# Splitting two of the second layer's seven products into seven smaller ones

## The chip, the cores and the metric

The kernel runs on one core of one Trainium2 chip. The metric is device time in microseconds (us) of one execution; of several executions the median is taken. TensorE multiplies, VectorE (DVE in the profile) and ScalarE (ACT) work element by element and can read the matmul accumulators in PSUM, GpSimd (POOL) works on SBUF, and SyncE's queue (SPq) issues the transfers (DMAs).

## What is computed

```python
kv  = einsum('bhsd,bhse->bhde', k, v)            # 8 batches, 8 heads, 576 tokens, 64 dims
att = einsum('bhsd,bhde->bhse', q, kv)
att = att / sqrt(mean(att*att, -1) + 1e-6) * g_norm
x   = att.transpose(0, 2, 1, 3).reshape(4608, 512)
h   = (1 / (1 + exp(-(x @ w_gate)))) * (x @ w_val)   # 4608 x 1536
out = h @ w_out                                      # 4608 x 512
```

Everything is float32.

## The kernel before, in words

**Chunks and stages.** The 4608 tokens are worked in nine chunks of 512 (`G`). Chunk 0 is multiplied plainly while the weights arrive. Chunks c = 1 to 8 each go through two stages: `first_layer_fast(c)` makes h (kept transposed, twelve tiles `gv[c, f]` of 128 features x 512 tokens), `second_layer_fast(c)` multiplies h by `w_out`. Both stages use a seven-product scheme (the one of Winograd and Strassen): a 2 x 2 block product is made with seven block products in place of eight, from sums of the operands' quarters and sums of the results.

**The second layer's operands.** The tokens of a chunk are two halves `h1`, `h2` of 256, the features two groups of six tiles (`lo` = f 0 to 5, `hi` = f 6 to 11), the 512 output columns two halves `d1`, `d2`. Three sums of `w_out`'s quarters are made once (`t2w`). The sums of h (`s12`, `s4`, and one quarter of `gv` overwritten by a difference) are made per f by VectorE in `h_sum` and `h_sums` (lines 844 to 856) as the first layer ends. All these tiles are of one pool of 21 buffers (`hp`, tag `gv`), which the k and v tiles of a later batch take too (`load_late`, line 105).

**The second layer's order.** For each g of two (128 of the 256 tokens of either half), seven products of six matmuls, each of 128 features x 128 tokens against 256 columns, accumulate in PSUM banks that `take` and `give` hand round (five banks). ScalarE copies or VectorE adds each result into `o1` or `o2`, two of the four `sg` buffers (`sg_tile`, line 480, 128 x 512 each; the first layer uses the same four, two per f, in turn). `store` (line 483) writes `o2` and `o1` of g = 0 in the middle of the stage and those of g = 1 near its end. A store of 128 tokens is two DMAs on SyncE's queue. For chunks whose rows lie in batch 2 or later, tokens are kept permuted, and a DMA has the form 32 x n rows with n from 1 to 3 (line 498); before that, it is one run of up to 128 rows (line 492). After the last store, `load_late(c + 2)` issues twelve DMAs for the k and v of a later batch; they are used by `kv_mm` (line 354), nine slots into the next first layer.

**The filler.** Attention for batch c + 1 is cut into steps and put into `fill` by `spread` (line 460). Each `slot()` in the matmul stream pops one step and emits it there, so that it takes its place in its engine's queue behind what was emitted before. The first layer has 42 slots, the second 28 (two per product). In the second layer of chunks 1 to 6 the slots hold, counted from 0: at 5 a TensorE step (`u_mm`, line 395), 6 and 9 ScalarE steps, 7 and 8 VectorE sums (line 404), 10 and 11 VectorE normalisations (line 413), 12 and 13 VectorE transposes (line 420), each followed by six DMAs from `xTs` to `xT` (line 430), 14 to 17 nothing, 18 the unpacking of `x_sums(c + 1)`, and 19 to 26 its eight VectorE sums (lines 691 to 694 of 512 columns, 701 to 704 of 128), the first of which reads what the DMAs of line 430 write. Chunk 7's eight sums lie in slots 1 to 8; chunk 8 has none. For chunk 1, twelve VectorE steps that make `t2w` are inserted too, every third place.

DMAs of SyncE's queue take eight completion semaphores in turn, so a DMA is issued only when the one eight before it has landed.

Of the kernel before, what the change touches and what calls it, by code (L numbers as in the profile page):

```python
# [15 lines left out]
ALU = mybir.AluOpType  # L16
# [4 lines left out]
def kernel(  # L21
# [11 lines left out]
    nc = tc.nc  # L33

    B, H, S, HD = q.shape
    T, DM = out.shape
    DF = moe_w_gate.shape[1]
    P = 128
# [22 lines left out]
    NFT = DF // P  # L61
    G = 512
    GH = G // 2
    NG = T // G
# [40 lines left out]
    def load_late(b):  # L105


        if b >= B:
            return
        mains = {}  # L110
        for n in range(NHP):
            for name, src in (("k", k), ("v", v)):
                mains[n, name] = t = hp.tile([P, G], FP32, tag="gv", name="kv")
                nc.sync.dma_start(out=t.rearrange("p (h c) -> p h c", h=2),
                                  in_=src[b, 2 * n:2 * n + 2, 0:S4].rearrange("h (p j) d -> p h (j d)", j=NK4))
        rest = hp.tile([P, G], FP32, tag="gv", name="kv")
        for i, src in enumerate((k, v)):
            for r in range(2):
                nc.sync.dma_start(out=rest[PH * r:PH * r + PH, GH * i:GH * i + GH].rearrange("p (h d) -> p h d", d=HD),
                                  in_=src[b, NHP * r:NHP * r + NHP, S4:S].rearrange("h p d -> p h d"))  # L120
        kv_late[b] = mains, rest
# [213 lines left out]
    def slot():  # L335
        if fill:
            fill.popleft()()
# [122 lines left out]
    def spread(steps, at):  # L460

        n = 0
        for engine, step in steps:
            while engine == DVE and n < 7 * NF2 and n % 7 not in at:
                fill.append(idle)
                n += 1
            fill.append(step)
            n += 1

    def flush():  # L470
        while fill:
            fill.popleft()()

    gv = {}
# [5 lines left out]
    def sg_tile():  # L480
        return sb.tile([P, G], FP32, tag="sg", name="sg", bufs=4)

    def store(c, t, ot, cols=slice(0, DM), queues=(nc.sync,)):

        r0 = i = 0
        while r0 < P:
            b, s = divmod(G * c + P * t + r0, S)
            rows = out[S * b:S * b + S, cols]
            if b < 2:
                j, p = divmod(s, NP)  # L490
                n = min(P - r0, NP - p)
                queues[i % len(queues)].dma_start(out=rows.rearrange("(p j) d -> j p d", j=NJ)[j, p:p + n],
                                                  in_=ot[r0:r0 + n, cols])
            else:
                half, c0 = divmod(s, S // 2)
                r, c0 = divmod(c0, XC)
                n = min(P - r0, XC - c0)
                queues[i % len(queues)].dma_start(
                    out=rows.rearrange("(r p g i) d -> i r g p d", p=QB, g=JH, i=2)[half, r, c0 // QB:(c0 + n) // QB],
                    in_=ot[r0:r0 + n, cols])  # L500
            r0 += n
            i += 1
# [7 lines left out]
    def bank(i):  # L510
        return (psum_mm if i < 2 else psum).tile([P, 512], FP32, tag=f"mm{i}", name="mm")
# [3 lines left out]
    def mm0_ps():  # L515
        return bank(next(turns0) % 2)

    def mm_ps():
        return bank((2, 3, 0, 1)[next(turns) % 4])

    def at_ps():
        return psum.tile([P, NQ, 512], FP32, tag="at", name="at")
# [4 lines left out]
    def take():  # L527
        i = free.popleft()
        return i, bank(i)[:, 0:GH]

    def give(i):
        free.append(i)

    def early(n):

        shared = []

        def ps(kind):
            if kind == "q":
                return shared[0]  # L540
            t = psum0.tile([P, 2, 512], FP32, tag="kq" if kind == "kv" else f"ux{n % 2}", name="two")
            if kind == "kv":
                shared.append(t)
                return t[:, :, JH * P:]
            return t
        return ps
# [33 lines left out]
    a = [attention(n, early(n)) for n in range(NE)]  # L580
# [19 lines left out]
    for token in order.split():  # L600
        name = token.rstrip("0123456789.")
        n = [int(i) for i in token[len(name):].split(".")]
        f = n[0]
        if name == "b":
            if f not in blks:
                if f == 3:
                    psum_ctx.__exit__(None, None, None)
                    psum = ctx.enter_context(tc.tile_pool(name="psum", bufs=1, space=bass.MemoryType.PSUM))
                    ps = (mm_ps(), mm_ps())
                else:  # L610
                    ps = (mm0_ps() if f else warm, mm0_ps())
# [29 lines left out]
    for f in range(4, NFT):  # L641
        if f == NFT - 1:
            last = at_ps()
# [6 lines left out]
    ps = [mm_ps() for _ in range(G // P)]  # L650
# [22 lines left out]
    NF2 = NFT // 2  # L673
    DH = DM // 2
    h1, h2 = slice(0, GH), slice(GH, G)
    tt = nc.vector.tensor_tensor
    sx, tw, s12, s4 = {}, {}, {}, {}
# [171 lines left out]
    def h_sums(c, f):  # L849
# [5 lines left out]
        tt(out=one[:, h2], in0=one[:, h1], in1=one[:, h2], op=ALU.subtract)  # L855
        tt(out=s4[c, f], in0=two[:, h1], in1=s[:, h2], op=ALU.subtract)

    def second_layer_fast(c):
        b = {(j, n): w2[:, NF2 * (j - 1):NF2 * j, DH * (n - 1):DH * n] for j in (1, 2) for n in (1, 2)}
        d1, d2 = slice(0, DH), slice(DH, DM)  # L860
        for g in range(2):
            t1, t2 = slice(P * g, P * g + P), slice(GH + P * g, GH + P * g + P)
            (i_a, pa), (i_b, pb) = (take() for _ in range(2))

            last = (c, g) == (NG - 1, 1)
            parts = [slice(0, DH // 2), slice(DH // 2, DH)] if last else [slice(0, DH)]

            def product(ps, hs, ws, new):
                for f in range(NF2):
                    nc.tensor.matmul(ps, hs(f), ws[:, f, :], start=(new and f == 0), stop=(f == NF2 - 1),  # L870
                                     skip_group_check=True)
                    if f % 3 == 2:
                        slot()

            product(pa, lambda f: gv[c, f][:, t1], b[1, 1], True)
            o2 = sg_tile()
            nc.scalar.copy(out=o2[:, d1], in_=pa)
            product(pb, lambda f: s12[c, f][:, t2], t2w[2], True)
            o1 = sg_tile()
            tt(out=o1[:, d2], in0=pb, in1=o2[:, d1], op=ALU.add)  # L880
            product(pa, lambda f: gv[c, f + NF2][:, t1], b[2, 1], False)
            nc.scalar.copy(out=o1[:, d1], in_=pa)
            if last:
                store(c, g, o1, d1)
            product(pb, lambda f: gv[c, f][:, t2], t2w[3], False)
            tt(out=o2[:, d2], in0=pb, in1=o2[:, d1], op=ALU.add)
            pcs = []
            for x in parts:
                i_c, pc = take()
                pc = pc[:, 0:x.stop - x.start]  # L890
                pcs.append((i_c, pc))
                product(pc, lambda f: s12[c, f][:, t1], t2w[1][:, :, x], True)
                o2x = o2[:, DH + x.start:DH + x.stop]
                tt(out=o2x, in0=pc, in1=o2x, op=ALU.add)
            product(pb, lambda f: gv[c, f + NF2][:, t2], t2w[4], False)
            tt(out=o2[:, d1], in0=pb, in1=o2[:, d1], op=ALU.add)
            store(c, 2 + g, o2)
            give(i_a)
            give(i_b)
            for (i_c, pc), x in zip(pcs, parts):  # L900
                give(i_c)
                product(pc, lambda f: s4[c, f][:, t1], b[2, 2][:, :, x], False)
                y = slice(DH + x.start, DH + x.stop)
                tt(out=o1[:, y], in0=pc, in1=o1[:, y], op=ALU.add)
                if last:
                    store(c, g, o1, y, (nc.sync, nc.scalar))
            if not last:
                store(c, g, o1)
            if g == 1:
                load_late(c + 2)  # L910

    def sums_of(c):
        if c < NG:
            fill.append(lambda: fill.extendleft(reversed(x_sums(c))))
# [17 lines left out]
    t2w = {i: sums.tile([P, NF2, DH], FP32, name=f"t2w{i}", bufs=1) for i in (2, 3, 4)}  # L932
# [14 lines left out]
    for c in range(1, NG):  # L947
        if c + 1 < B:
            steps = feed(c + 1)
            if c == 1:  # L950

                i = 4
                while w2_sums:
                    steps.insert(i, (DVE, w2_sums.popleft()))
                    i += 3
            spread(steps, (1, 2, 3, 4, 5) if c == 1 else (2, 3, 4, 5))
        first_layer_fast(c)
        sums_of(c + 1)
        second_layer_fast(c)
        flush()  # L960
# [30 lines left out]
```

## Time and profile before

| | us |
|---|---|
| median of 3 runs | 1078.0 (1076.03 to 1078.93) |
| the profiled execution, its own time | 1075.73 |
| its span, first to last instruction | 1073.9 |
| a second layer (chunks 2 to 5), TensorE busy without a gap over 150 ns | 38.3 |
| a second layer of chunk 8, which has no filler | 36.5 |
| VectorE busy in a second layer (chunks 2 to 5) | 17.2 |
| GpSimd busy in a second layer (chunks 2 to 5) | 4.5 |

A line of the profile names an engine, a source line, an operation, what it writes and reads, and the shapes. In the timeline each line has start and duration in us, and in brackets the idle time of that engine before it and what ended it. One matmul of float32 appears as two MATMUL records.

### The profile page before, as it was taken

The numbers are of one execution on the slowest core, as the hardware profiler recorded it, in microseconds if no ns is written. First come the engines' busy times: TensorE is split into PE (matmuls) and PEld (weight loads), VectorE is DVE, ScalarE is ACT, GpSimd is POOL, SyncE is SP. The second block draws the span as 40 slices with busy tenths as digits, with TensorE's granted clock in tenths as the row PEclk, the third lists the DMA queues.
The fourth block names the chain that finished last, engine by engine and source line by source line (L and its number), as shares of the span: only waits on it lengthen the run. The fifth ranks groups of instructions, "written<-read, shape, count | busy, mean of one in ns | idle before, by whom it ended". The sixth has DMA issues, their size and how long they took to land.

```text
span 1073.9 us, 19464 instructions
## 1 busy us (share of the span) xinstructions
PE 1062.2 (99%) x7514; PEld 882.4 (82%) x7514; DVE 712.0 (66%) x1461; ACT 309.0 (29%) x737; POOL 442.1 (41%) x630
## 2 busy tenths in 40 slices
PE   8999999999999999999999999999999999999997
PEld 7544448888888888888888888888888888888886
DVE  4897767894579547863778357945786388628841
ACT  4654323331243113320433134312431122112210
POOL 0000035880367216640666046713663077307800
PEclk9999999999999999999999999999999999999999
DMA  9944710002400141012301140014001200010001
GB/s 259 254 157 157 244 29 22 24 17 60 119 12 13 45 128 36 12 35 62 100 23 34 42 120 13 25 45 137 13 12 27 58 2 1 2 38 1 1 1 40
DMA packets 69115, 64.96 MB, mean 60 GB/s; under 512 B 23712, under 2 KB 63008, under 8 KB 69024
## 3 DMA queue, kind: packets, MB, share of 16 engines
q1 hardware_dynamic: 68768, 63.69, 21.1%
q8 instruction: 60, 0.98, 0.4%
q14 instruction: 31, 0.25, 0.1%
q10 hardware_dynamic: 256, 0.03, 0.1%
HBM read 47.19 MB, written 9.44 MB: 53 GB/s over the span
## 4 chain that ended last, share of the span: by engine, by line
PE 97%; DVE 1%; DMA 1%; SPq 0%; issue 0%; ACT 0%; DVEq 0%
PE mm L728 46%; PE mm L870 27%; PE mm L732 7%; PE mm L556 7%; PE mm L653 4%; PE at L395 2%; PE at L354 1%; PE at L556 1%; DMA q<-in_q_dram 1%; PE two L291 0%; PE two L261 0%; PE mm L634 0%; PE two L318 0%; PE two L272 0%; PE at L360 0%; SPq L97 0%
## 5 line engine op out<-in xcount | busy, mean ns | idle before, releaser
L720 POOL TENSOR_TENSOR tw<-gv 128x256 f32<-128x256 f32 x192 | 156.2, 823 | 232.1 <-DVE w L202 145.0
L728 PE MATMUL mm<-xT,tw 128*128 128x256 f32 x768 | 198.4, 381 | 0.0
L728 PE MATMUL mm<-sx,tw 128*128 128x256 f32 x768 | 197.4, 380 | 0.0
L802 POOL TENSOR_TENSOR sg<-sg 128x256 f32<-128x256 f32 x48 | 35.6, 742 | 341.1 <-ACT sg L801 340.9
L720 POOL TENSOR_TENSOR tw<-gv,tw 128x256 f32<-128x256 f32 x192 | 155.0, 828 | 0.0
L728 PEld LDWEIGHTS mm<-xT,tw 128*128 128x128 f32 x768 | 137.3, 190 | 17.5 <-issue 2.9
L728 PEld LDWEIGHTS mm<-sx,tw 128*128 128x128 f32 x768 | 134.9, 191 | 12.4
L773 DVE TENSOR_TENSOR gv<-gv,sg 128x256 f32<-128x256 f32 x192 | 108.7, 585 | 0.0
L728 PE MATMUL mm<-sx,gv 128*128 128x256 f32 x384 | 91.2, 380 | 0.0
L728 PE MATMUL mm<-xT,gv 128*128 128x256 f32 x384 | 90.8, 379 | 0.0
L870 PE MATMUL mm<-w,gv 128*128 128x256 f32 x384 | 89.1, 381 | 0.7 <-DVE gv L773 0.7
L870 PE MATMUL mm<-t2w,gv 128*128 128x256 f32 x384 | 88.7, 381 | 0.0
L870 PE MATMUL mm<-w,s 128*128 128x256 f32 (+1 forms) x408 | 88.3, 367 | 0.0
L764 ACT ACTIVATE sg<-sg 128x256 f32<-128x256 f32 x96 | 40.0, 416 | 151.0 <-DVE sg L763 150.9
L739 ACT COPY sg<-mm 128x256 f32<-128x256 f32 x96 | 35.8, 373 | 162.7 <-PE mm L728 160.9
L870 PEld LDWEIGHTS mm<-w,gv 128*128 128x128 f32 x384 | 72.5, 190 | 12.2 <-DVE gv L773 2.5
L870 PEld LDWEIGHTS mm<-w,s 128*128 128x128 f32 x408 | 74.1, 190 | 9.4
L728 PEld LDWEIGHTS mm<-xT,gv 128*128 128x128 f32 x384 | 72.9, 190 | 10.4 <-issue 0.5
L728 PEld LDWEIGHTS mm<-sx,gv 128*128 128x128 f32 x384 | 72.5, 190 | 10.0
L870 PEld LDWEIGHTS mm<-t2w,gv 128*128 128x128 f32 x384 | 72.4, 190 | 10.0
L556 PE MATMUL mm<-xT,gv 128*128 128x512 f32 x176 | 77.4, 594 | 0.0
L745 DVE TENSOR_TENSOR gv<-mm,sg 128x256 f32<-128x256 f32 x96 | 37.0, 413 | 41.2 <-PE mm L728 37.8
(120 smaller groups left out, 1548.4 us busy)
## 6 DMA issues: line engine op xcount, KB each, us to landing
q<-in_q_dram SPq DMA_DIRECT2D x24, 288.0 KB
st<-in_moe_w_gate_dram SPq DMA_DIRECT2D x12, 512.0 KB
st<-in_moe_w_val_dram SPq DMA_DIRECT2D x12, 512.0 KB
st<-in_moe_w_out_dram SPq DMA_DIRECT2D x12, 512.0 KB
kv<-in_k_dram SPq DMA_DIRECT2D x24, 256.0 KB
kv<-in_v_dram SPq DMA_DIRECT2D x24, 256.0 KB
out_dram<-sg SPq DMA_DIRECT2D x23, 192.0 KB
xT<-xTs SPq DMA_DIRECT2D x48, 72.0 KB
```

The source lines that it names most:

```text
L395: nc.tensor.matmul(u[HD * e:HD * e + HD, r, o:o + HD], qTs[QB * r:QB * r + QB, (n0 + which) % 2, c:c + PH], kvq[QB * r:QB * r + QB, (n0 + ...
L556: nc.tensor.matmul(self.ps[i], w[("wg", "wv")[i], self.f][:, m, :], xT[self.c][:, m, :], start=(m == 0), stop=(m == NMT - 1), skip_group_c ...
L653: nc.tensor.matmul(ps[t], gv[0, f][:, P * t:P * t + P], w["wo", f], start=(f == 0), stop=(f == NFT - 1), skip_group_check=True)
L720: nc.gpsimd.tensor_tensor(out=tw[f, i], in0=b[in0], in1=b[in1] if isinstance(in1, tuple) else tw[f, in1], op=ALU.subtract)
L728: nc.tensor.matmul(ps, wt[:, m, :], xs[:, m, :], start=(new and m == 0), stop=(m == NK - 1), skip_group_check=True)
L732: nc.tensor.matmul(ps, wt, xs, start=new, stop=True, skip_group_check=True)
L739: nc.scalar.copy(out=d["sg"][:, h2], in_=d["pa"])
L745: tt(out=d["h"][:, h1], in0=d["pb"], in1=d["sg"][:, h2], op=ALU.add)
L764: nc.scalar.activation(out=d["sg"][:, h2], in_=d["sg"][:, h2], func=AF.Sigmoid)
L773: tt(out=d["h"][:, h], in0=d["h"][:, h], in1=d["sg"][:, h], op=ALU.mult)
L802: nc.gpsimd.tensor_tensor(out=g2[:, h1], in0=g2[:, h1], in1=g2[:, h2], op=ALU.add)
L870: nc.tensor.matmul(ps, hs(f), ws[:, f, :], start=(new and f == 0), stop=(f == NF2 - 1), skip_group_check=True)
```

## The change

Of the seven products per stage, two are no longer made as one: the one that went into `o1[:, d1]` (`gv` hi, tokens of `h1`, with the quarter `b[2, 1]` of `w_out`), and the one that went into `o2[:, d1]` (`gv` hi, tokens of `h2`, with `t2w[4]`). Each is split once more in seven (`split`), on blocks of 3 feature tiles x 128 tokens x 128 columns, so it takes 21 matmuls of 128 columns for both g together in place of 12 of 256.

The sums that this needs are made per chunk by `sums2`: of the two quarters of `w_out` on GpSimd (`tw4`, `tw2_`, twelve operations of 128 x 128 each), of h on VectorE (`sa4`, `sa2`, twelve each). They overwrite parts of `gv` and `s12` tiles whose last reader has been emitted.

The other five products are now emitted in pairs over g, so that all four of `o1`, `o2` are alive until the splits, which come last: `split(o2)`, the stores of both `o2`, `split(o1)`, the stores of both `o1`, then `load_late`. In the last chunk the `d2` halves of `o1` are stored before the last split, and the `d1` halves in pieces after it. Slots per stage stay 28: 0 to 19 in the ten large products, 20 to 23 in `split(o2)`, 24 to 27 in `split(o1)`. The `t2w` steps of chunk 1 are inserted every second place.

```diff
+    N3 = NF2 // 2
+    d1, d2 = slice(0, DH), slice(DH, DM)
+    tok = [slice(P * i, P * i + P) for i in range(G // P)]
+    def sums2(engine, x, out, weights):
+        o = dict(zip((1, 2, 4, 3), out))
+        if weights:
+            ops = ((1, (1, 2), (1, 1)), (2, (2, 2), 1), (4, (2, 1), 2), (3, (2, 2), (1, 2)))
+        else:
+            o[3] = x[2, 1]
+            ops = ((1, (2, 1), (2, 2)), (2, 1, (1, 1)), (3, (1, 1), (2, 1)), (4, (1, 2), 2))
+        for i, in0, in1 in ops:
+            for j in range(N3):
+                u0, u1 = (x[n][j] if isinstance(n, tuple) else o[n][j] for n in (in0, in1))
+                engine.tensor_tensor(out=o[i][j], in0=u0, in1=u1,
+                                     op=ALU.add if i == 1 and not weights else ALU.subtract)
+        return o
...
-        for g in range(2):
...
-            product(pa, lambda f: gv[c, f + NF2][:, t1], b[2, 1], False)
-            nc.scalar.copy(out=o1[:, d1], in_=pa)
...
-            product(pb, lambda f: gv[c, f + NF2][:, t2], t2w[4], False)
-            tt(out=o2[:, d1], in0=pb, in1=o2[:, d1], op=ALU.add)
-            store(c, 2 + g, o2)
...
+        for g in pair:
+            i_, pa = take()
+            product(pa, of(gv, lo, g), b[1, 1], True)
+            o2[g] = sg_tile()
+            nc.scalar.copy(out=o2[g][:, d1], in_=pa)
+            give(i_)
+        tw4 = sums2(nc.gpsimd, b4, thirds(of(gv, lo, 0) + of(gv, lo, 1)), True)
+        for g in pair:
+            i_b[g], pb[g] = take()
+            product(pb[g], of(s12, lo, 2 + g), t2w[2], True)
+            o1[g] = sg_tile()
+            nc.scalar.copy(out=o1[g][:, d1], in_=o2[g][:, d1])
+            tt(out=o1[g][:, d2], in0=pb[g], in1=o2[g][:, d1], op=ALU.add)
+        sa4 = sums2(nc.vector, a4, thirds(of(s12, lo, 2) + of(s12, lo, 3))[:3], False)
+        for g in pair:
+            product(pb[g], of(gv, lo, 2 + g), t2w[3], False)
+            tt(out=o2[g][:, d1], in0=pb[g], in1=o2[g][:, d1], op=ALU.add)
+            give(i_b[g])
+        sa2 = sums2(nc.vector, a2, thirds(of(gv, lo, 2) + of(gv, lo, 3))[:3], False)
+        for g in pair:
+            i_c[g], pc[g] = take()
+            product(pc[g], of(s12, lo, g), t2w[1], True)
+            tt(out=o2[g][:, d2], in0=pc[g], in1=o2[g][:, d1], op=ALU.add)
+        tw2_ = sums2(nc.gpsimd, b2, thirds(of(s12, lo, 0) + of(s12, lo, 1)), True)
+        for g in pair:
+            product(pc[g], of(s4, lo, g), b[2, 2], False)
+            tt(out=o1[g][:, d2], in0=pc[g], in1=o1[g][:, d2], op=ALU.add)
+            give(i_c[g])
+        def split(o, x, a, sa, w_, tw_, done=None):
+            (i_d, pd), (i_e, pe), (i_f, pf), (i_h, ph) = (take() for _ in range(4))
...
+            small(pd, a[1, 1], w_[1, 1], True)
+            add(o[0][:, l], pd)
+            small(pf, a[1, 2], w_[2, 1], True)
+            add(o[0][:, l], pf)
+            slot()
+            small(pd, sa[2], tw_[2], False)
+            add(o[0][:, r], pd)
+            small(pe, sa[1], tw_[1], True)
+            add(o[1][:, r], pe)
+            slot()
+            small(pd, sa[3], tw_[3], False)
+            y = o[1][:, x].rearrange("p (n c) -> p n c", n=2)
+            tt(out=y, in0=y, in1=pd.unsqueeze(1).to_broadcast([P, 2, P]), op=ALU.add)
+            small(ph, a[2, 2], tw_[4], True)
+            add(o[1][:, l], ph)
+            slot()
+            if done:
+                done()
+            small(pe, sa[4], w_[2, 2], False)
+            add(o[0][:, r], pe)
+            slot()
...
+        split(o2, d1, a4, sa4, b4, tw4)
+        for g in pair:
+            store(c, 2 + g, o2[g])
+        if ends:
+            for g in pair:
+                store(c, g, o1[g], d2)
+            split(o1, d1, a2, sa2, b2, tw2_, lambda: [store(c, 1, o1[1], d1), store(c, 0, o1[0], tok[0])])
+            store(c, 0, o1[0], tok[1], (nc.sync, nc.scalar))
+        else:
+            split(o1, d1, a2, sa2, b2, tw2_)
+            for g in pair:
+                store(c, g, o1[g])
+        load_late(c + 2)
...
-                    i += 3
+                    i += 2
```

More of the change, by code (lines that the diff above doesn't have):

```diff
@@ L858, in second_layer_fast @@
     def second_layer_fast(c):
         b = {(j, n): w2[:, NF2 * (j - 1):NF2 * j, DH * (n - 1):DH * n] for j in (1, 2) for n in (1, 2)}
-        d1, d2 = slice(0, DH), slice(DH, DM)
-        for g in range(2):
[L862 to L870, printed above, removed]
-                                     skip_group_check=True)
[L872 to L880, printed above, removed]
-            product(pa, lambda f: gv[c, f + NF2][:, t1], b[2, 1], False)
-            nc.scalar.copy(out=o1[:, d1], in_=pa)
[L883 to L894, printed above, removed]
-            product(pb, lambda f: gv[c, f + NF2][:, t2], t2w[4], False)
-            tt(out=o2[:, d1], in0=pb, in1=o2[:, d1], op=ALU.add)
-            store(c, 2 + g, o2)
[L898 to L910, printed above, removed]
@@ new lines, in second_layer_fast, with product, of, thirds @@
+        ends = c == NG - 1
+        pair = range(2)
+        lo, hi = range(NF2), range(NF2, NFT)
+        def product(ps, hs, ws, new):
+            for f in range(NF2):
+                nc.tensor.matmul(ps, hs[f], ws[:, f, :], start=(new and f == 0), stop=(f == NF2 - 1),
+                                 skip_group_check=True)
+                if f % N3 == N3 - 1:
+                    slot()
+        def of(tiles, fs, t):
+            return [tiles[c, f][:, tok[t]] for f in fs]
+        def thirds(tiles):
+            return [tiles[i:i + N3] for i in range(0, len(tiles), N3)]
@@ new lines, in h_quarters, with w_quarters @@
+        def h_quarters(tiles, fs, t):
+            return {(i, k): of(tiles, fs[N3 * (k - 1):N3 * k], t + i - 1) for i in (1, 2) for k in (1, 2)}
+        def w_quarters(ws):
+            return {(k, n): [ws[:, f, tok[n - 1]] for f in range(N3 * (k - 1), N3 * k)] for k in (1, 2) for n in (1, 2)}
+        a4, a2 = h_quarters(gv, hi, 2), h_quarters(gv, hi, 0)
+        b4, b2 = w_quarters(t2w[4]), w_quarters(b[2, 1])
+        o2, o1, pb, pc, i_b, i_c = {}, {}, {}, {}, {}, {}
+        for g in pair:
[4 more added lines that the diff above has]
+            give(i_)
@@ new lines, in split, with small, add @@
+        def split(o, x, a, sa, w_, tw_, done=None):
+            (i_d, pd), (i_e, pe), (i_f, pf), (i_h, ph) = (take() for _ in range(4))
+            pd, pe, pf, ph = (ps[:, 0:P] for ps in (pd, pe, pf, ph))
+            l, r = slice(x.start, x.start + P), slice(x.start + P, x.stop)
+            def small(ps, hs, ws, new):
+                for j in range(N3):
+                    nc.tensor.matmul(ps, hs[j], ws[j], start=(new and j == 0), stop=(j == N3 - 1),
+                                     skip_group_check=True)
+            def add(t, ps):
+                tt(out=t, in0=ps, in1=t, op=ALU.add)
+            small(pd, a[1, 1], w_[1, 1], True)
[18 more added lines that the diff above has]
+            add(o[0][:, r], pe)
+            slot()
+            for i in (i_d, i_f, i_h, i_e):
+                give(i)
```

## The prediction, on record before the changed kernel ran

> **What bounds the kernel now.** The page comes first: TensorE is busy for the whole span and is nearly all of the chain that ended last.
>
> ```profile
> PE 1062.2 (99%) x7514; PEld 882.4 (82%) x7514; DVE 712.0 (66%) x1461; ACT 309.0 (29%) x737; POOL 442.1 (41%) x630
> ...
> PE 97%; DVE 1%; DMA 1%; SPq 0%; issue 0%; ACT 0%; DVEq 0%
> ```
>
> So a microsecond less of TensorE's work is a microsecond less of time, if nothing makes TensorE wait. What a product costs stands in TensorE's timeline of the last second layer (start, duration). The last product there is already made in two halves of 128 columns:
>
> ```profile
> 1055.20 2.75 PE L870 MATMUL mm<-t2w,gv 128*128 128x256 f32 x12
> ...
> 1057.79 2.84 PE L870 MATMUL mm<-w,s 128*128 128x128 f32 x24
> ...
> 1060.47 2.75 PE L870 MATMUL mm<-t2w,gv 128*128 128x256 f32 x12
> ```
>
> From start to start: six matmuls of 256 columns take 2.59 us (0.432 each), twelve of 128 take 2.68 (0.223 each). Back to back, small ones cost only 0.015 us more than half a large one.
>
> Next VectorE in chunk 2's second layer, which runs from 352.56 to 390.90:
>
> ```profile
> 378.22 0.42 DVE L880 TENSOR_TENSOR sg<-mm,sg 128x256 f32<-128x256 f32 x1 [4.82 <-PE mm L870]
> 382.59 0.69 DVE L691 TENSOR_TENSOR sx<-xT 128x512 f32<-128x512 f32 x1 [3.94 <-DMA xT<-xTs]
> 383.31 0.69 DVE L692 TENSOR_TENSOR sx<-sx,xT 128x512 f32<-128x512 f32 x1
> 383.92 0.68 DVE L693 TENSOR_TENSOR xT<-xT 128x512 f32<-128x512 f32 x1
> 384.52 0.42 DVE L886 TENSOR_TENSOR sg<-mm,sg 128x256 f32<-128x256 f32 x1
> ```
>
> VectorE sits at the head of its queue until the xT transfers land; the addition of a finished product (L886) waits behind. It hurts nobody today, as no product needs that bank for 2.6 us. Then SyncE's queue and the DMA rate:
>
> ```profile
> 370.83 1.27 SPq L498 DMA_DIRECT2D out_dram<-sg  x2
> 372.20 9.74 SPq L430 DMA_DIRECT2D xT<-xTs  x12
> 382.04 0.98 SPq L492 DMA_DIRECT2D out_dram<-sg  x2
> ```
>
> ```profile
> 383.00:384.50 1.50, 1.50 (x9) 1.32 (x8) 1.47 (x3) 0.00 (x0) 0.00 (x0) 1.00 0.61 175
> 1052.00:1054.00 2.00, 2.00 (x11) 1.77 (x10) 0.42 (x1) 0.00 (x0) 0.00 (x0) 1.00 0.19 56
> 1066.00:1069.00 3.00, 0.00 (x0) 0.00 (x0) 0.23 (x1) 0.00 (x0) 0.00 (x0) 1.00 0.32 53
> 1069.00:1072.40 3.40, 0.00 (x0) 0.00 (x0) 0.00 (x0) 0.00 (x0) 0.00 (x0) 0.56 0.15 43
> ```
>
> The last columns are granted clock, DMA share of 16 engines, GB/s. A 256 KB store in the form of line 492 (first row) moves at 175 GB/s; the form of line 498 (second row) at 56 with 3 of 16 engines (0.19 x 16). After TensorE stops at 1065.9, stores still drain for over 6 us. Last, ScalarE at the start of the next first layer (it starts at 390.90):
>
> ```profile
> 392.87 0.37 ACT L739 COPY sg<-mm 128x256 f32<-128x256 f32 x1 [0.54 <-PE mm L728]
> 393.14 0.27 ACT L791 COPY sg<-mm 128x128 f32<-128x128 f32 x1
> ```
>
> These write the `sg` buffers that the previous stage's first two results had.
>
> [...]
>
> **TensorE's work.** A split takes 21 x 0.223 = 4.69 us in place of 12 x 0.432 = 5.18. Two splits per stage: -0.98; in chunk 8 the old halves go too: 36.45 before, 10 x 2.59 + 42 x 0.223 = 35.27 after. Seven stages and the last: -6.9 - 1.2 = **-8.1 us**, the whole possible gain.
>
> **Hand-offs within a split.** The third small product adds into the bank that the first addition has to read, with one product (3 x 0.223 = 0.67 us) between. From the trace: an addition starts 0.20 after its product's last issue slot, takes 0.29 (L894), TensorE restarts 0.05 later and loses 0.11 (as after the wait at 239.99): 0.65. It just fits; with a 0.69 us sum between, 0.1 to 0.2 is lost. I take **+1.5** for 32 such places (0 to 6).
>
> **GpSimd's sums.** 24 per stage at 0.48 to 0.64 us (L713), 6 us a stream. The first runs from 5.2 to about 11.5 us of the stage, is needed at 29; the second from 22.7 to 29 (both after GpSimd's 4.5 us rest of weight sums) and is needed at 34. VectorE's sums lie between. Hidden: 0; uncovered, 6 us a stage.
>
> **VectorE's sums and the xT wait, chunks 1 to 6.** 24 sums of 128 columns at a pitch of 0.20 us (L702 to L703, 386.26 to 386.46): 4.8 us per stage; VectorE is busy 17.2 of 38.3, so no bound. But twelve stand before slot 8's sum and twelve before slot 12's transposes. In chunk 2's clock: `sa4` 365.5 to 368.0, then slot 8's sum to 368.7, an addition to 369.05, root and normalisations to 370.8, an addition to 371.15, `sa2` to 373.55, transpose to 374.3 (before: 371.5), and xT's first DMA leaves at 374.35, 21.8 us into the stage (before 19.6, held by a store until then). From first DMA to L691 it took 7.7 to 10.4 in chunks 1 to 6, longest beside slow stores; with none beside it 8.0: L691 at 29.8. The ten large products end at 27.98, two small ones at 29.3; the third needs the first addition, which now stands in VectorE's queue behind L691 (0.6), a large addition (0.34) and itself (0.29), plus 0.16: 31.2. Stall 1.9 us (0.7 with sums that hide, 4 with sums at 0.35), x6: **+11.4**.
>
> **Stores and sg.** All four stores now leave at the end. With E the end of TensorE's stage, `o2`'s first DMA goes at E-4.0 (end of `split(o2)` at E-4.7, addition, 0.6). Its data start 1.2 later. By line 498 a store is either 32+96 rows[...] or 64+64[...]. The pair of 370.83 needed 7.6 us to its last packet, one of 32+96 (388.96) 4.7; behind another 3 and 5.5 more. Chunks 3 and 6[...]: second `o2` landed at E+3.7. Chunks 2, 4, 5, 7[...]: E+6.5. Chunk 1 has line 492's form: no wait. But the second copy of the next first layer (392.87 above: E+1.97) needs exactly that buffer, and the next copy (393.14) is awaited by TensorE's matmul at E+3.04. So TensorE restarts 0.8 after the landing: stall 3.7 + 0.8 - 3.04 = 1.45, twice, and 4.25, four times: **+19.9** (14 to 28).
>
> **k and v.** SyncE reaches `load_late` about 1.2 us later, and its DMAs wait for semaphores of `o1`'s stores, which land at about E+10 to E+17[...]. Today kv_mm comes at E+16.4, the last load at about E+14.6 to E+15.9. New about E+17.7 to E+22; part lies under the sg stall. **+3** in all (0 to 9).
>
> **The end.** [...] Before: 1072.3, E+6.5. **+8.9** (5 to 11).
>
> **Sum.** -8.1 + 1.5 + 11.4 + 19.9 + 3 + 8.9 = +36.6 on the profiled 1075.7 (span 1073.9 and 1.8 around it), 1112.3; the runs' median is 2.3 above that execution: 1078.0 + 36.6 = **1115**.
>
> **The rivals.** *Faster:* all stays covered. The deciding point is `o2`'s second store landing before E+2.2 and L691 starting before 27.9; if stores overlap on different engines (1.5 us each, as in line 492's form), TensorE's saving is all that is left: 1078 - 8.1 = 1070. For it: 99% busy and 21 us of free VectorE per stage; against: the 56 GB/s. *Only VectorE's wait:* stores land in time, -8.1 + 1.5 + 11.4 + 3 (SyncE's thirteen last issues at 0.6): 1086. *VectorE late and clock lost:* sums at 0.35 us add 3.6 us to each of six waits, hand-offs lose 0.2 each: about 1140; the same follows where 4.25 us stalls halve the clock for the next few us.
>
> **Chances.** Main case 0.60 (own range 1103 to 1128), VectorE late or clock lost 0.15, only VectorE's wait 0.12, between the last and the main one 0.05, faster 0.05, cancelling out 0.03. Range 1092 to 1140 leaves out the lower three. About 0.3% is what a measurement of this kernel can tell from no change: faster 0.05, same 0.03, slower 0.92.
>
> **What would show it.** Right: L739 copies ended by a DMA early in chunks 2 to 7's successors, with TensorE idle 1 to 5 us about 3 us into them; TensorE idle about 2 us after the sixth small matmul, released by VectorE behind L691; over 15 us of transfers after the last matmul. Wrong: line 498's stores above 100 GB/s, or small products pitched at over 0.23 us.

## The result, and the profile after

| | before | after |
|---|---|---|
| median, us | 1077.07 | 1146.28 |
| ratio to before | | 1.0642 (1.062 to 1.0665) |
| profiled execution, own time / span, us | 1075.73 / 1073.9 | 1146.46 / 1144.7 |
| last matmul to the end of the span, us | 8.0 | 14.1 |

The change makes the kernel 69 us slower. The direction was forecast; the size was not (1115, with 1140 as the upper end of the range).

The page of the changed kernel, the lines that answer to those of before:

```profile
PE 1081.7 (95%) x7778; PEld 900.8 (79%) x7778; DVE 801.9 (70%) x1747; ACT 307.5 (27%) x737; POOL 529.6 (46%) x822
...
PEclk9999999999999989999999899998999999989997
...
PE 82%; DVE 8%; DMA 5%; SPq 2%; issue 1%; ACT 1%; DVEq 0%; POOL 0%; ACTq 0%; POOLq 0%
```

TensorE's share of the chain falls from 97% to 82%; VectorE and transfers take what it lost. The row of granted clocks (one digit per fortieth of the span, 9 for 90% of full speed or more) shows five slices of 8 or 7; the same row of the kernel before has 9 in all forty.

**Where TensorE stands still.** Its timeline through chunk 2's second layer (356.37 to 399.14) and the start of the next first layer:

```profile
377.66 1.68 PE L888 MATMUL mm<-w,s 128*128 128x256 f32 x7
382.18 7.01 PE L888 MATMUL mm<-w,s 128*128 128x256 f32 x24 [2.84 <-DVE sg L932]
389.02 1.50 PE L947 MATMUL mm<-t2w,gv 128*128 128x128 f32 x12
390.91 1.35 PE L947 MATMUL mm<-gv,s 128*128 128x128 f32 x10 [0.38 <-DVE sg L951]
```

```profile
404.13 0.49 PE L732 MATMUL mm<-xT,gv 128*128 128x128 f32 x2 [2.88 <-ACT sg L739]
404.46 1.03 PE L728 MATMUL mm<-sx,tw 128*128 128x256 f32 x4
406.99 0.80 PE L732 MATMUL mm<-sx,tx 128*128 128x128 f32 x2 [1.50 <-ACT sg L791]
407.58 0.64 PE L732 MATMUL mm<-xT,tx 128*128 128x128 f32 x2
```

Three kinds of gap. The one of 2.84 us was not in the prediction: the first `s4` product accumulates into the bank of the first `t2w1` product, and waits until the addition after that one (L932) has read it. The one of 0.38 is the predicted wait behind the xT transfers, in the third product of `split(o2)`. The two at the start of the first layer are the predicted wait for the `sg` buffers, seen from ScalarE, whose two copies are each released by a store:

```profile
403.71 0.37 ACT L739 COPY sg<-mm 128x256 f32<-128x256 f32 x1 [30.84 <-DMA out_dram<-sg]
406.39 0.37 ACT L739 COPY sg<-mm 128x256 f32<-128x256 f32 x1 [2.31 <-DMA out_dram<-sg]
406.66 0.27 ACT L791 COPY sg<-mm 128x128 f32<-128x128 f32 x1
```

Before, the same copy ran 1.97 us after the stage began (392.87); here it is 7.25 us (406.39 less 399.14).

**Why the addition is late.** VectorE, then GpSimd, in the same stretch of chunk 2:

```profile
374.87 5.48 DVE L876 TENSOR_TENSOR gv<-gv 128x128 f32<-128x128 f32 x12
380.27 1.54 DVE L420 STREAM_TRANSPOSE xTs<-sqs 128x288 f32<-128x288 f32 x4
381.74 0.71 DVE L932 TENSOR_TENSOR sg<-mm,sg 128x256 f32<-128x256 f32 x2
```

```profile
374.67 1.38 POOL L876 TENSOR_TENSOR s<-w 128x128 f32<-128x128 f32 x3 [8.49 <-PE mm L888]
376.02 2.80 POOL L876 TENSOR_TENSOR s<-w,s 128x128 f32<-128x128 f32 x6
378.78 1.42 POOL L876 TENSOR_TENSOR s<-w 128x128 f32<-128x128 f32 x3
```

GpSimd's second stream runs from 374.67 to 380.20, the very time of VectorE's second twelve sums. Those take 5.48 us. The first twelve of the same shape, which run from 369.35 with GpSimd idle (it stands still from 366.17 to 374.67), take 2.50. The kernel before has the same in small, at the start of chunk 2's second layer, where three sums of one shape follow one another on VectorE; GpSimd's line comes last:

```profile
355.50 0.94 DVE L854 TENSOR_TENSOR s<-s,gv 128x256 f32<-128x256 f32 x1
356.37 0.94 DVE L855 TENSOR_TENSOR gv<-gv 128x256 f32<-128x256 f32 x1
357.24 0.41 DVE L856 TENSOR_TENSOR s<-gv,s 128x256 f32<-128x256 f32 x1
```

```profile
355.26 1.77 POOL L720 TENSOR_TENSOR tw<-gv,tw 128x256 f32<-128x256 f32 x2
```

The two that begin before GpSimd's sums end, at 357.03, take 0.94 us each, the one behind them 0.41.

**The clock.** Two stretches of the next first layer, the first behind the gaps (the column before the last two is the granted clock, x counts the matmul records):

```profile
407.00:412.60 5.60, 5.60 (x16) 4.79 (x17) 1.36 (x4) 2.40 (x5) 1.19 (x2) 0.50 0.76 246
413.00:418.60 5.60, 5.60 (x30) 4.99 (x29) 3.93 (x11) 1.14 (x3) 3.12 (x6) 1.00 0.45 116
```

TensorE is busy in both, but 16 records fall into the first and 30 into the second. Ten windows of half clock, of 3.41 or 6.83 us each, lie ahead of the last matmul; the kernel before has none there.

**The sum of the profile after.** Over the span, +70.8 us: gaps of TensorE behind L932's addition 19.1 (2.84 in each of chunks 1 to 6, 1.0 in 7 and 8), behind the xT transfers 3.3, for `sg` 24.2 (chunks 2 to 7); half-clock windows 47.8, of which 8.9 lie inside gaps, so (47.8 - 8.9) / 2 = 19.4 lost; the end +6.1; TensorE's work -6.7. That is 65.4. The -6.7 takes the 0.82 us by which chunk 7's stage gets shorter for each of seven stages, and 1.0 for chunk 8. The last kernels below, which have no such waits left, show chunks 2 to 6 saving only 0.1 to 0.4 each, so about 2 of the other 5.4 us belong there. Another 3 or so stand in the first layers of chunks 3 to 8, about half a microsecond in each beyond its gaps and its half clock; their cause stays open.

### The profile page after: what moved, and what is told of

It is laid out like the page before. It is cut to its first block, busy times and chain, and to the rows that moved or that the text cites. A ratio compares the mean times of both kernels' runs of the same rounds, so it can differ in the third digit from the quotient of the medians.

```text
span 1144.7 us, 20611 instructions
## 1 busy us (share of the span) xinstructions
PE 1081.7 (95%) x7778; PEld 900.8 (79%) x7778; DVE 801.9 (70%) x1747; ACT 307.5 (27%) x737; POOL 529.6 (46%) x822
## 4 chain that ended last, share of the span: by engine, by line
PE 82%; DVE 8%; DMA 5%; SPq 2%; issue 1%; ACT 1%; DVEq 0%; POOL 0%; ACTq 0%; POOLq 0%
PE mm L728 43%; PE mm L888 11%; PE mm L732 7%; PE mm L556 7%; DMA out_dram<-sg 5%; PE mm L947 4%; DVE gv L876 4%; PE mm L653 4%; PE at L395 2%; SPq L430 1%; PE at L354 1%; DVE s L876 1%; PE mm L634 1%; DVE sqs L413 1%; SPq L498 1%
## 5 line engine op out<-in xcount | busy, mean ns | idle before, releaser
L728 PE MATMUL mm<-sx,tw 128*128 128x256 f32 x768 | 205.6, 392 | 0.0
L728 PEld LDWEIGHTS mm<-sx,tw 128*128 128x128 f32 x768 | 140.7, 199 | 13.5
L888 PE MATMUL mm<-w,s 128*128 128x256 f32 x384 | 92.7, 402 | 19.1 <-DVE sg L932 19.1
L888 PEld LDWEIGHTS mm<-w,s 128*128 128x128 f32 x384 | 77.0, 202 | 33.5 <-DVE sg L932 22.3
L728 PEld LDWEIGHTS mm<-xT,gv 128*128 128x128 f32 x384 | 72.5, 190 | 9.9 <-issue 0.5
L763 DVE TENSOR_TENSOR sg<-mm,sg 128x256 f32<-128x256 f32 x96 | 40.6, 423 | 30.8 <-PE mm L728 30.5
L556 PEld LDWEIGHTS mm<-xT,gv 128*128 128x128 f32 x176 | 32.7, 190 | 37.3 <-issue 35.8
L749 DVE TENSOR_TENSOR gv<-mm,gv 128x256 f32<-128x256 f32 x96 | 40.3, 420 | 29.6 <-PE mm L728 28.5
L713 POOL TENSOR_TENSOR tx<-gv,tx 128x128 f32<-128x128 f32 x96 | 53.3, 556 | 7.5
```

What stands on the lines that cost most here:

```text
L556: nc.tensor.matmul(self.ps[i], w[("wg", "wv")[i], self.f][:, m, :], xT[self.c][:, m, :], start=(m == 0), stop=(m == NMT - 1), skip_group_c ...
L713: nc.gpsimd.tensor_tensor(out=tw2[i], in0=in0, in1=tw2[in1] if isinstance(in1, int) else in1, op=ALU.subtract)
L728: nc.tensor.matmul(ps, wt[:, m, :], xs[:, m, :], start=(new and m == 0), stop=(m == NK - 1), skip_group_check=True)
L749: tt(out=d["h"][:, h2], in0=ps, in1=d.pop("u")[:, h2], op=ALU.add)
L763: tt(out=d["sg"][:, h2], in0=d["pb"], in1=d["sg"][:, h2], op=ALU.add)
L888: nc.tensor.matmul(ps, hs[f], ws[:, f, :], start=(new and f == 0), stop=(f == NF2 - 1), skip_group_check=True)
```

## The experiments

The theory: two waits do the harm, one behind VectorE's sums, which take 5.48 us in place of 2.50 beside GpSimd's, and one for slow stores (0.18 of the DMA engines) holding the `sg` buffers; the gaps then cost clock on top (windows at 0.50). The rivals: VectorE just has too much queued, the stores are late and not slow, and the half clock is no cost of its own.

**The late stream.** The outputs of GpSimd's second stream are written in the reverse order, so that the first one lies where the pair's last matmuls read.

```diff
-        tw2_ = sums2(nc.gpsimd, b2, thirds(of(s12, lo, 0) + of(s12, lo, 1)), True)
+        tw2_ = sums2(nc.gpsimd, b2, thirds(of(s12, lo, 0) + of(s12, lo, 1))[::-1], True)
```

> The changed kernel with the second stream of w_out sums on GpSimd writing its outputs in the reverse order, so that its first output waits for the last matmuls of the t2w1 pair and the stream no longer runs beside VectorE's second twelve sums (sa2). Theory (the two streams block each other): sa2 takes 2.5 us per stage in place of 5.5, TensorE's gap of 2.84 us before the second s4 product falls under 0.3 in chunks 1 to 6 and the one of 1.0 in chunks 7 and 8 to nothing (19.1 us in all to under 2), the wait of the splits for the xT transfers falls from 3.3 us in all to under 1, some half-clock windows go: about 1120 us. Rival (VectorE simply has too many operations queued ahead of that addition, whatever GpSimd does): sa2 gets shorter but at least 1.5 us of gap stay per stage, over 1135 us.

Measured: 1123.83 us, 1.0455 (1.0425 to 1.0484). VectorE's timeline, the same stretch of chunk 2, and GpSimd's first line:

```profile
373.50 2.50 DVE L876 TENSOR_TENSOR gv<-gv 128x128 f32<-128x128 f32 x12
375.92 1.55 DVE L420 STREAM_TRANSPOSE xTs<-sqs 128x288 f32<-128x288 f32 x4
377.40 0.38 DVE L932 TENSOR_TENSOR sg<-mm,sg 128x256 f32<-128x256 f32 x1
```

```profile
377.19 1.31 POOL L876 TENSOR_TENSOR s<-w 128x128 f32<-128x128 f32 x3 [12.39 <-PE mm L888]
```

The twelve sums are back at 2.50 us in all eight stages, and the gap behind L932 is gone in all of them. The rival falls: the queue is as long as before, only the overlap with GpSimd's sums is gone. (The expectation puts the gap before the second `s4` product; in the trace it stands before the first.) The xT wait did not fall as expected; it rose from 3.3 to 8.3 us, as TensorE now arrives there without having waited earlier. So of 19 us, 5 came back one wait later. The half-clock windows fell from 47.8 to 27.3 us, and the time by 22 us in all.

**Stores of 32 rows.** One line of `store`, in the branch for batch 2 and later:

```diff
-                n = min(P - r0, XC - c0)
+                n = min(P - r0, QB)
```

> The changed kernel with its stores cut into DMAs of 32 rows each[...]; nothing else. Theory (four bunched stores[...] hold the sg buffers that the next first layer needs): the two gaps at the start of each of six first layers, 24 us in all, go; the half-clock windows that begin there (about 34 us at half speed) go with them; the end after the last matmul falls from 14.1 to about 9 us: about 1104 us. Rival (the first copy waits for the stores because they are issued late, not because they are slow): the gaps stay at 1 us or more in each of six stages, over 1125 us.

Measured: 1104.61 us, 1.0261 (1.0248 to 1.0274). ScalarE at the start of the first layer after chunk 2 (which begins at 400.6):

```profile
401.65 0.37 ACT L739 COPY sg<-mm 128x256 f32<-128x256 f32 x1 [27.35 <-PE mm L728]
402.84 0.37 ACT L739 COPY sg<-mm 128x256 f32<-128x256 f32 x1 [0.81 <-DMA out_dram<-sg]
403.11 0.27 ACT L791 COPY sg<-mm 128x128 f32<-128x128 f32 x1
```

The first copy now waits for its product only; the second still for a store, but 2.2 us into the stage in place of 7.25, which TensorE does not feel: no gap over 150 ns is left at the start of any first layer. The first store is issued as late as before (at 396.46, 4.1 us ahead of the stage's end; in the changed kernel at 395.02, 4.1 ahead too), so they were slow, not late. The DMA columns of two stretches shortly after that issue, the changed kernel first:

```profile
396.50:398.50 2.00, 2.00 (x20) 2.00 (x20) 1.20 (x4) 0.00 (x0) 0.00 (x0) 1.00 0.18 45
397.50:399.50 2.00, 2.00 (x20) 2.00 (x20) 1.18 (x6) 0.00 (x0) 0.00 (x0) 1.00 0.52 129
```

A share of 0.18 is three engines of 16 on average (0.18 x 16 = 2.9), one of 0.52 more than eight (8.3); the rate rises from 45 to 129 GB/s. The half-clock windows at the starts of the first layers (34.1 us) are gone, as expected; four of 3.41 stay in the second layers. The end after the last matmul is 10.6 us. The gaps behind L932 are still 19.1 us in all: the two waits are independent.

**Both edits.**

> Both edits together: the late second stream on GpSimd and the stores of 32 rows. If the two waits are independent and nothing else stands behind them, all gaps over 0.3 us are gone from the second layers and from the starts of the first layers, the granted clock stays at 1.0 until the last matmul, and the time is 1075 to 1082 us. If a third wait stands behind them (the loads of k and v, or the hand-offs of the split), it stays above 1090 us and the trace shows where.

Measured: 1082.35 us, 1.0056 (1.0043 to 1.0069). All windows of half clock ahead of the last matmul are gone. The time lies just above the expected range, which left out the wait for xT. That wait is what is left of gaps (us in total, times, longest):

```profile
PE mm L947 <- DVE sg L951: 7.9, 6, 2.0
```

It falls in chunks 1 to 6. Neither k and v nor the hand-offs of the split show as gaps.

**The kernel before with stores of 32 rows.** The same line of `store`, nothing else.

> The kernel before with the same stores of 32 rows. It shows what the stores alone are worth without the split. Theory: the kernel before has no wait for its stores inside, so only the end after the last matmul gets shorter, 8.0 us to 5 or 6: 1074 to 1076 us, 0.998 of before. Rival: the doubled number of DMA issues on SyncE's queue delays the xT or k and v transfers and costs 2 us or more.

Measured: 1072.21 us, 0.9965 (0.9956 to 0.9975). That is below the expected range: the end after the last matmul falls from 8.0 to 4.0 us, more than was put, and this is the whole difference of the medians (1076.18 to 1072.21), 0.35%. The rival falls. The end is read from a profiled execution of 1076.33 us, in which chunk 1's second layer begins 4.0 us later than before (240.98 for 236.96); its total is therefore not compared.

**The sums of x later.** On top of both edits, two more empty steps at the end of the attention's steps:

```diff
-        return steps + two_pairs(n0 + 2) + [(PE, idle)] * 4
+        return steps + two_pairs(n0 + 2) + [(PE, idle)] * 6
```

> Both edits of before (late second stream, stores of 32 rows) and the eight sums of x two slots later, so that the first one, which waits for the xT transfers, stands behind the fourth addition of the first split and not ahead of its first. Theory (that wait, 0.5 to 2.0 us in each of chunks 1 to 6, 7.9 us in all, is what is left inside the stages): the gaps fall to under 1.5 us in all and the time to 1075 to 1077 us. Rival (xT lands so late that the wait only moves two products further): gaps of 0.5 us or more stay in at least four stages, over 1079 us.

Measured: 1074.88 us, 0.9988 (0.998 to 0.9996). Gaps over 60 ns inside the second layers add up to 0.7 us. With every long wait gone, the split kernel is at last no slower than the one before, but it carries the better stores too and is still above the 1072.21 of the kernel before with them.

**The last chunk as before.** On top, chunk 8's second layer is the old one.

```diff
-        second_layer_fast(c)
+        (second_layer_plain if c == NG - 1 else second_layer_fast)(c)
```

> As the one with the sums of x later, but the last chunk's second layer is that of the kernel before. Theory: the end after the last matmul falls from 10.6 us to the 4.0 of the kernel before with stores of 32 rows, and TensorE has 1.0 us more to do: 5.6 us less, 1069 to 1072 us, at or below the 1072.2 of the kernel before with those stores, by what the seven other stages save (0.8 us each at most). Rival (the hand-offs inside the splits eat the saving of TensorE): 1073 us or more.

Measured: 1069.05 us, 0.9936 (0.9923 to 0.995), the fastest; the interval lies below that of the old kernel with the new stores (0.9956 to 0.9975). The page:

```profile
PE 1059.6 (99%) x7766; PEld 885.5 (83%) x7766; DVE 770.0 (72%) x1713; ACT 307.9 (29%) x737; POOL 514.2 (48%) x798
...
PE 98%; DMA 0%; SPq 0%; issue 0%; DVE 0%; ACT 0%
```

So the split, with the two changes of order that it needs, is worth 3.2 us over the old kernel with the same stores. Chunk 7's stage, whose only filler is eight sums in slots 1 to 8, gets 0.82 us shorter (35.44 for 36.26); seven times that would be 5.7. But chunks 2 to 6 take 37.92 to 38.21 us for 38.34, only 0.13 to 0.42 less. Part of what is lost there stands in `split(o1)`: in chunk 2 its second small product takes 0.92 us from start to start, in chunk 7 0.67. So the rival of this run, hand-offs that eat the saving, is right in part.

**Matmuls in the gap.** On the changed kernel, six matmuls whose result nobody reads, between the `t2w1` and the `s4` pair.

```diff
+        i_w, pw = take()
+        for _ in range(6):
+            nc.tensor.matmul(pw, ident, b[1, 1][:, 0, :], start=True, stop=True)
+        give(i_w)
```

> The changed kernel with six matmuls of 256 columns, 2.6 us, whose result nobody reads, between the t2w1 pair and the s4 pair, where TensorE stands still for 2.84 us (chunks 1 to 6) or 1.0 us (7 and 8). Theory (the gaps also cost a granted clock of half for 3.4 us afterwards): the gap falls to about 0.25 us in chunks 1 to 6, the stage gets no longer for it there, 1.6 us longer in chunks 7 and 8, and the windows of half clock that begin at this gap (four of six stages) go: 1146 - 4 x 1.6 + 3 = about 1143 us. Rival (the half clock is only a mark of the gap and costs nothing of its own): 1149 us or more, as the added matmuls lengthen the last two stages and give nothing back.

Measured: 1149.38 us, 1.0682 (1.0668 to 1.0697), the rival's number. Yet the total does not decide. All windows of half clock behind this gap are gone, as the theory has it. But in chunks 1 and 2 the xT wait grew to 2.0 us each (from 0.55 and 0.38), which took the gain back there; chunks 7 and 8 got 1.3 us longer each, and the first layers 1.5 us longer in all. The single stages do decide, by the change of the gap, of the added work (2.59) and of the xT wait. In chunks 3 and 6, which had no window of half clock behind the gap, these three give -0.94 and 0.0 us, and the stages changed by -0.94 and 0.0. In chunks 4 and 5, which had one of 3.41 us, they give +0.7 each, and the stages got 0.84 and 1.16 us shorter: 1.6 and 1.8 us, about half of the window, went with it.

**A short and a long gap on the fastest kernel.** ScalarE repeats one copy at the start of the first layers of chunks 2 to 8.

```diff
-            nc.scalar.copy(out=g1[:, q1], in_=pd[:, q1])
+            for _ in range(22 if c > 1 and f == 0 else 1):
+                nc.scalar.copy(out=g1[:, q1], in_=pd[:, q1])
```

(10 in place of 22 for the short gap.)

> The fastest kernel so far (1069.05 us: late second stream, stores of 32 rows, later sums of x, last chunk as before) with ScalarE repeating one copy of 128 columns ten times at the start of the first layers of chunks 2 to 8, where in the changed kernel TensorE waited for the sg buffers. It makes one gap per stage, of about 9 x 0.23 - 1.1 = 1 us. Theory (a gap costs its own length[...]): the gaps add up to about 7 us, no window of half clock, 1069 + 7 = 1076 us. Rival (any gap costs a restart of 1 us or more beyond its length): 1083 us or more.

> The same with 22 copies, one gap of about 21 x 0.23 - 1.1 = 3.7 us per stage. Theory (long gaps also halve the clock for 3.4 us or more afterwards): gaps of 26 us in all and a window of half clock behind most of them, 1.7 us each or more: 1069 + 26 + 12 = about 1107 us, 8 us or more beyond the sum of the gaps. Rival (half clock is only a mark and costs nothing): 1069 + 26 = 1095 us.

Measured: short 1090.01 us, 1.0132 (1.0112 to 1.0151); long 1126.29, 1.0462 (1.0446 to 1.0477). The gaps came out longer than I had worked out, since repeated copies stand 0.28 to 0.30 us apart and not 0.23. Short: seven gaps of 2.0 to 2.5, 14.8 us in all, span +19.4 against the fastest kernel; two windows of half clock of 3.41, 3.4 us lost, where none was expected. 14.8 + 3.4 = 18.2 of 19.4, so a restart of 1 us per gap, the rival, is not in it, although the time lies above the rival's number. Long: seven gaps of 5.55 to 6.0, 39.3 us in all, span +56.5; seven windows of 6.83, of which 14.6 of 47.8 us lie inside gaps, so 16.6 lost. 39.3 + 16.6 = 55.9 of 56.5. TensorE behind one long gap and a little later:

```profile
406.10:410.60 4.50, 4.50 (x14) 3.87 (x15) 0.85 (x2) 1.46 (x4) 0.70 (x1) 0.50 0.78 230
411.00:415.00 4.00, 4.00 (x22) 3.59 (x21) 3.12 (x9) 0.54 (x2) 1.91 (x3) 1.00 0.20 53
```

14 records in 4.5 us against 22 in 4.0. Half clock is a cost of its own, and it is paid for half of the window's time outside the gap. The rival, with the gaps that came out, would stand at 1069 + 39.3 = 1108 us; it falls by 18.

**When a gap halves the clock.** The traces record when the granted clock changes. In each of them all windows of half clock start whole multiples of 3.413 us apart, the length of the shortest of them: in the changed kernel at 262.50, 381.96 and 405.86, which is 35 and 7 such steps on. The clock is 0.50 from 262.50 to 265.91 and 1.00 in the 3.41 us on either side. So in these traces it seems to be not the length of a gap that counts, but how much of it falls into one of these steps. The gaps of 2.84 us in chunks 1, 2, 4 and 5 left TensorE idle for 2.42, 2.63, 2.02 and 2.01 us of one step, and half clock followed from the next one on; in chunks 3 and 6 the same gap straddled two steps, at most 1.97 and 1.87 us fell into one, and the clock stayed full. Over all eleven traces, after the first 20 us, half clock followed each of the 32 steps at full clock with 2.01 us or more of idle time (as the profile has it, which models the ends of matmuls), and only two of the 3357 with less (1.81 and 1.95 us); in the changed kernel alone, each of nine, and one of 302 (1.81). No run was made to test this border; it is read from the traces afterwards.

## Why the prediction was wrong

The direction was right, and two waits came as forecast (for xT and for `sg`); one forecast wait, for k and v, did not come, and 34 us were missing between its +36.6 and the profile's +70.8. By its steps:

- **TensorE's work and hand-offs**, -8.1 + 1.5 = -6.6: right for the stages of chunks 7 and 8 (0.82 and 1.0 less), where the product that adds into a bank just read is pitched at 0.71 us in place of 0.67: the 0.65 of the hand-off fits almost, as worked out. In chunks 2 to 6, with the filler, only 0.13 to 0.42 is saved once the long waits are gone. Over the eight stages of the kernel with the later sums of x that makes about -4.7, so this term was 2 us too good.
- **GpSimd's sums**, "The second from 22.7 to 29 ... VectorE's sums lie between. Hidden: 0": **the step that failed.** I let the second stream wait for the end of the `t2w1` pair, since it overwrites what that pair reads. But it overwrites it tile by tile, and its first outputs are the tiles read first: it started 18.3 us into the stage, 0.2 us ahead of `sa2`. What GpSimd's sums do to VectorE's stood in the trace of the kernel before (L854 took 878 ns in the mean of 48, L856, of the same shape, 0.41 us at 357.24, with GpSimd's sums ended), but by my schedule the two did not overlap. They did: 2.50 us became 5.48, twelve sums at a pitch of 0.45. Price: 19.1 us of gaps and the four half-clock windows of the second layers. The late stream shows it. My own schedule left the addition that it hit no margin. Carried on from the prediction's transpose at 374.3, a second transpose (0.75) and the addition (0.3) end at 375.35, and the `s4` pair was to begin at 352.56 + 22.7 = 375.3 (an estimate from the prediction's own figures). So 3 us more of `sa2` became a gap of 2.84 almost undiminished.
- **VectorE's wait for xT**, +11.4: 3.3 in the changed kernel, 7.9 to 8.3 once the other wait was gone. The mechanism was right, the price about two fifths too high, and waits in series on one engine do not add up: the earlier one had already been paid.
- **Stores and sg**, +19.9: gaps of 24.2 us, and the mechanism as put. In chunks 2, 4, 5 and 7 the gaps are 3.3 to 5.4 us for 4.25 predicted (after chunk 2 the copy that waits for the deciding landing runs at E+7.25; the landing was put at E+6.5, an estimate of mine). In chunks 3 and 6, for which E+3.7 and 1.45 us were predicted, they are 3.0 and 3.1, and that is most of what was missing. Stores of 32 rows took it all away: with only the form of the DMA changed, the share of busy DMA engines rose from 0.18 to 0.52. Which engines a store's rows go to was not shown; the 3 and 5.5 us that one was to take behind another were my estimate.
- **k and v**, +3: nothing; TensorE never waited for them. SyncE did wait for the landing of stores ahead of them, as forecast, but hardly more than before (line 114, 10.4 us in all in nine waits for 9.4 in six; the queue's 385 DMAs take eight semaphores in turn, 47 to 49 each). The landings at E+10 to E+17 were my estimate.
- **The end**, +8.9: +6.1. The forecast was an estimate of mine; how the last stores share the engines was not shown.
- **Half clock**: the second step that failed. It was put into a rival at 0.15 with "VectorE late", and priced at nothing in the main case. It was 19.4 us. The kernel before showed half clock only behind its last matmul (0.56 in 1069 to 1072.4, with TensorE idle since 1065.9), so what a gap of 4.25 us, forecast in four stages, does to the clock was not shown then. In the changed kernel windows of 3.41 and 6.83 us came with about 2 us of idle in the 3.41 ahead of them (2.01 to 2.94 in nine of the ten, 1.81 in one).

Missing, then: 19.1 behind VectorE's slowed sums, 19.4 for the clock, 4.3 for sg and 5.4 of small pieces, less 8.1, 3 and 2.8 that were put too high. "VectorE late or clock lost" (about 1140) was the nearest of the cases. That it came so near is in part luck: it priced one or the other at about 25 us, and with another reason for the first (slower sums in the wait for xT); both came, at 19 us each.

## What to carry to other kernels

Where an engine overwrites what another reads, find the first element it overwrites and that element's last reader, not the end of the whole read: that is when the stream starts, and what it will run beside. Cost the waits of a bound engine in their order, as the first one pays part of the next. Add half the clock window (3.41 or 6.83 us in these traces, less what lies inside the gap) behind each gap that can leave 2 us idle within 3.41 us: by the border of 2.01 us in these traces a gap of 2 to 4 us does so or not as it happens to fall, one of over 4 us always (an estimate from the 2.01 and the 3.413: cut in two, it still leaves over 2 in one step), and two short gaps close together can do it too (1.21 and 1.75 us did). A change of order moves transfers as well: what was spread over a stage and is now bunched at its end has to be costed at the share of the DMA engines that it gets there (0.18 for these stores).

## What the runs showed of the hardware that I had not expected

- Gaps of 2.84 us halved TensorE's clock in four of six stages, gaps of 2.0 to 2.5 us in two of seven, and 1.21 and 1.75 us 1.35 apart did so together (529.21 and 532.31 in the changed kernel). In these traces it goes with whether about 2.0 us of idle fall into one of the steps of 3.413 us on which the windows start. Windows lasted one or two such steps, 3.41 or 6.83 us, as long as TensorE went on working.
- Cutting two stores of 128 rows into eight DMAs of 32 rows in place of four takes longer on SyncE's queue (3.77 us against 2.65) and still brought the copy that waits for their landing forward by 5 us (7.25 to 2.2 us into the stage), at a DMA share of 0.52 in place of 0.18.
- VectorE and GpSimd, each adding 128 x 128 float32 from SBUF, ran VectorE at a pitch of 0.45 us in place of 0.20, and GpSimd hardly slower (5.53 us for twelve beside those sums, 5.03 in the late stream, away from them). In this pairing VectorE pays.
